# q's weight halves laid 226 columns apart, each with its gate column behind it

## The chip, the cores and the metric

The kernel runs on one core of a Trainium2 chip. The metric is the device time of one execution in microseconds. Three runs of the kernel before gave 392.96, 392.97 and 393.01 us (median 392.97). One more execution, taken with the profiler on, took 392.84 us; its span, from the first to the last recorded instruction, is 391.1 us.

## The reference

Inputs are float32: x of 2048 x 448, the attention's `wqkv` (448 x 1344) and `wo` (448 x 448), the MLP's `w1` (448 x 1792), `b1`, `w2` (1792 x 448) and `b2`, and a gate vector of 448.

```python
g = _sigmoid((x * gate_w).sum(-1, keepdims=True))
a = _A_ref(x, A_wqkv, A_wo)
b = _B_ref(x, B_w1, B_b1, B_w2, B_b2)
return g * a + (1 - g) * b
```

`_A_ref` is attention with 16 heads of 28 numbers: each position looks at itself and at seven earlier positions in steps of two, and the result goes through `wo`. `_B_ref` is `relu(x @ w1 + b1)**2 @ w2 + b2`. What matters here is the first step of `_A_ref`, `qkv = x @ wqkv`, and the gate's dot product of x and `gate_w`. The kernel computes that as one more column of the products with q's weights.

## The kernel before

**Precision and tiles.** Every float32 operand is split into a high part, rounded to the format `fp32r`, and a low part, the rest. A product x·w is the sum of three products on TensorE: high·high, high·low, low·high. The 448 rows of a weight are three blocks of 128 rows (k = 0, 1, 2) and one of 64. For the last block q's weights take partitions 0 to 63 of `w7h` and `w7l`, k's take partitions 64 to 127 of the same columns. The 2048 positions are four chunks of 512, and a chunk is four tiles of 128 positions. x is the stationary operand and the weights are the moving one, so a product's duration goes with the columns of the weights.

**The woven reading.** `woven` (L190) makes the moving operand's access pattern: it takes the columns alternately from two halves (column n of the first half, column n of the second, then n + 1 of both), and `woven_out` (L196) names the output's columns accordingly. For a weight of 448 columns the halves lie 224 columns apart. q's weights have NQ = 450 columns: 448, and twice the gate's column behind them. With halves 224 apart, the gate's column at 448 is reached as number 224 of the second half, and number 224 of the first half is column 224 itself, read a second time. `NH = D // 2 + 2` makes 226 pairs, so that these products have 452 output columns; `qkv_evacuate` takes the gate's value from output column 449 (`pt[:, D + 1:D + 2]`, L369).

**The start.** An order written out by hand stands in L801 to L843. Nineteen products on zeros run first on TensorE. Meanwhile q's weights, `raws[0]`, arrive block by block on SP's queue and x's first chunk in `rx`. For each block k (L830 to L839) ScalarE copies the 450 columns into `wqh` (the high part), VectorE subtracts that from the raw numbers into `wql` (the low part), and both split x in the same way. L840 to L843 do this for the last block. GpSimd has only fills to do at this time (L239, L241, L306).

**The products.** `qkv_first` (L420) runs q's products of chunk 0 in the order in which the blocks come in: for each of the three blocks of 128 rows, over four tiles, high·high, low weights, low x (L429, 36 products on all 128 rows). All later products go through `side_by_side` (L334): each uses 64 rows of the array, and a pair, one in each half of the array, runs at the same time on two different tiles (L341). The last block of q (`last`, L398) runs in pairs with k's. In chunks 1 to 3 `qkv_two` (L447) does two tiles per call in 63 pairs; in such a call the first half has 24 products of q and the second 18, never in the same pair, and the partner is always one of k or v with 448 columns.

**What sets the order behind it.** From L846 on a planner (`Plan`) gives each engine its order at build time from written costs and start times (`START`, `FIRST`, `MM448`). The times are constants in the code, so the planner's order does not depend on how the weights are laid out. `x_load` (L705) brings the next chunks of x into the two buffers of the pool `rawp`; the first of them is the one that held `raws[0]`.

Of the kernel before, what the change touches and what calls it, by code (L numbers as in the profile page):

```python
# [9 lines left out]
AF = mybir.ActivationFunctionType  # L10
# [3 lines left out]
S, D, H, DH, W, F = 2048, 448, 16, 28, 8, 1792  # L14
# [7 lines left out]
NF = F // P  # L22
CH = 512
NQ = D + 2
NH = D // 2 + 2
NP = 512


# [155 lines left out]
def gated_mix_kernel(ctx: ExitStack, tc: tile.TileContext, xT, wqkv, w1, w2, wo, b1, b2, out):  # L184
    nc = tc.nc

    def f32(ap):
        return ap.bitcast(F32)

    def woven(w):  # L190

        if w.shape[1] == NQ:
            return bass.AP(tensor=w.tensor, offset=w.offset, ap=[list(w.ap)[0], [1, NH], [D // 2, 2]])
        return w.rearrange("p (i n) -> p n i", i=2)

    def woven_out(pt, n):  # L196
        return (pt[:, :2 * NH] if n == NQ else pt[:, :n]).rearrange("p (n i) -> p n i", i=2)

# [81 lines left out]
    def x_slot(j, o=16):  # L280
        return x_place[0][:, o + 2 * CH * j:o + 2 * CH * (j + 1)].rearrange("p (i n) -> p i n", i=2)

    def x_tiles(c):
        if c % 2:
            x_place[0] = xpool.tile([P, 8 * CH + 16], F32R, tag="x", name=f"x{c}")
            return [x_slot(j, 0 if c == 1 else 16) for j in range(4)]
        return [xap.tile([P, 2, CH], F32R, tag=f"x{j}", name=f"x{c}_{j}") for j in range(4)]
# [9 lines left out]
    ap = actx.enter_context(tc.tile_pool(name="phase_a", bufs=1, reuse_waits="tile"))  # L297
    xap = actx.enter_context(tc.tile_pool(name="phase_a_x", bufs=1, reuse_waits="tile"))
    wqh = ap.tile([P, 3, NP + 2 * D], F32R, name="wqh")
    wql = ap.tile([P, 3, NP + 2 * D], F32R, name="wql")  # L300
    w7h = ap.tile([P, NP + D], F32R, name="w7h")
    w7l = ap.tile([P, NP + D], F32R, name="w7l")
# [10 lines left out]
    def ncols(b):  # L313
        return NQ if b == 0 else D

    def block(b):
        o = (0, NP, NP + D)[b]
        return slice(o, o + ncols(b))
# [15 lines left out]
    def side_by_side(*todo):  # L334
        assert len(todo[0]) == len(todo[1])
        for pair in zip(*todo):
            need(*(j for e in pair for j in (*e[0].after, *e[3:])))
            for r, (acc, a, w, *_) in enumerate(pair):
                rows = slice(r * 64, r * 64 + 64)
                assert acc.rows in (None, r)  # L340
                nc.tensor.matmul(woven_out(acc.pt, acc.n), a[rows], woven(w[rows]), start=acc.todo == acc.all, stop=acc.todo == 1)  # L341
                acc.todo, acc.rows, acc.after = acc.todo - 1, r, ()
            plan.pe(MM512 if pair[0][0].n == CH else MM448 + (pair[0][0].n - D) * 1.7)
# [41 lines left out]
    def wqj(b, k):  # L385
        return wq_jobs.get((b, k), ())
# [10 lines left out]

    def last(x, acc, tl, b):  # L398
        sl = slice(tl * P, tl * P + P)
        n = block(1) if b == 2 else slice(0, ncols(b))  # L400
        h, l = w7h[:, n], w7l[:, n]
        (wh, wl), (xh, xl) = (wqj(2, 3) if b == 2 else ()) or (None, None), x.parts[3] or (None, None)
        return [(acc, x.x7[:, sl], h, *filter(None, (wh, xh))), (acc, x.x7[:, sl], l, *filter(None, (wl,))),
                (acc, x.x8[:, sl], h, *filter(None, (xl,)))]
# [15 lines left out]
    def qkv_first(x):  # L420
        four = range(4)
        q = accs(0, 0, four, "bbbb")
        for k in range(3):
            todo = [full(x, q[i], i, 0, (k,)) for i in four]
            for some in ((0, 1), (2, 3)) if k == 0 else (four,):
                for j in range(3):
                    for i in some:
                        acc, a, w, *_ = todo[i][j]
                        nc.tensor.matmul(woven_out(acc.pt, NQ), a, woven(w), start=k == j == 0, stop=False)  # L429
            plan.pe(FIRST[k])  # L430
        for acc in q:
            acc.todo = 3
        k = accs(0, 1, four, "mmmm")
        t = [sum((last(x, a[i], i, b) for i in four), []) for b, a in ((0, q), (1, k))]
        f = [full(x, k[i], i, 1) for i in four]
        run(0, [t[0] + f[0] + f[1] + f[2] + f[3], t[1] + f[2] + f[3] + f[0] + f[1]],
            [(3, [(0, 0, q[0])], (k[0], k[0])),
             (12, [(0, i, q[i]) for i in (1, 2, 3)], (k[1], k[1])),
             (24, [], (k[0], k[2])), (33, [], (k[1], k[3])),
             (39, [(1, 0, k[0]), (1, 2, k[2])]), (48, [(1, 1, k[1]), (1, 3, k[3])])])  # L440
        v = accs(0, 2, four, "bbbb")
        f, l = [full(x, v[i], i, 2) for i in four], [last(x, v[i], i, 2) for i in four]
        run(0, [f[0] + l[0] + f[2] + l[2] + f[1] + f[3], f[1] + l[1] + f[3] + l[3] + f[0] + f[2]],
            [(15, [], (v[0], v[1])), (24, [], (v[2], v[3])),
             (33, [(2, 0, v[0]), (2, 1, v[1])]), (42, [(2, 2, v[2]), (2, 3, v[3])])])

    def qkv_two(x, c, t0, beside=()):  # L447
        t1 = t0 + 1
        kinds = ("mm", "bm", "bb") if beside else ("mm", "mb", "bb")
        (q0, q1), (k0, k1), (v0, v1) = (accs(c, b, (t0, t1), tags) for b, tags in enumerate(kinds))  # L450
        run(c, [full(x, q0, t0, 0) + last(x, q0, t0, 0) + full(x, q1, t1, 0) + last(x, q1, t1, 0) + full(x, k0, t0, 1)
                + full(x, k1, t1, 1) + full(x, v0, t0, 2) + last(x, v0, t0, 2) + full(x, v1, t1, 2),
                full(x, k1, t1, 1) + last(x, k1, t1, 1) + full(x, v0, t0, 2) + full(x, v1, t1, 2) + last(x, v1, t1, 2)
                + full(x, q0, t0, 0) + full(x, q1, t1, 0) + full(x, k0, t0, 1) + last(x, k0, t0, 1)],
            [(24, [], (q0, k1)), (33, [], (q1, v0)), (42, [(0, t0, q0), (1, t1, k1)], (k0, v1)),
             (51, [(0, t1, q1)]), (51, [], *beside[:1]), (54, [(2, t0, v0)]), (57, [], *beside[1:]),
             (63, [(1, t0, k0), (2, t1, v1)])])
# [351 lines left out]
    raws = [rawp.tile([P, 4, 512], F32, tag="raw", name="wqraw0")]  # L809
# [12 lines left out]
    for b, tag in ((1, "k"), (2, "v")):  # L822
        raw = attp.tile([P, 3, D], F32, tag=tag, name=f"wqraw{b}")
# [3 lines left out]
    raw7 = attp.tile([P, D], F32, tag="q", name="wqraw7")  # L827
    nc.sync.dma_start(raw7, wqkv[2, :, 3, :D])
    x = X(x_tiles(0))
    for k in range(3):  # L830
        nc.scalar.activation(wqh[:, k, :NQ], raws[0][:, k, :NQ], AF.Copy)
        for n, cols in enumerate(halves if k == 0 else (slice(0, CH),)):
            if k or n:
                nc.scalar.activation(x.h[k][:, cols], rx[:, k, cols], AF.Copy)
            else:
                nc.vector.tensor_copy(x.h[k][:, cols], rx[:, k, cols])
            if not n:
                nc.vector.tensor_sub(wql[:, k, :NQ], raws[0][:, k, :NQ], f32(wqh[:, k, :NQ]))
            nc.vector.tensor_sub(x.l[k][:, cols], rx[:, k, cols], f32(x.h[k][:, cols]))  # L839
    nc.scalar.activation(w7h[:, :NQ], raws[0][:, 3, :NQ], AF.Copy)  # L840
    nc.vector.tensor_sub(w7l[:, :NQ], raws[0][:, 3, :NQ], f32(w7h[:, :NQ]))
    nc.scalar.activation(x.x7, rx[:, 3], AF.Copy)
    nc.vector.tensor_sub(x.x8, rx[:, 3], f32(x.x7))  # L843

# [304 lines left out]
    def wo_end(st):  # L1149
        for r in range(2):  # L1150
            for e in wo_full(st, r, (0, 1, 2)):
                acc, a, w, *js = e
                need(*acc.after, *js)
                nc.tensor.matmul(woven_out(acc.pt, D), a, woven(w), start=False, stop=acc.todo == 1)  # L1154
                acc.todo, acc.after = acc.todo - 1, ()
                plan.pe(MM448)
            fin_add(st.par, st.t + r, acc, gt[:, st.par, st.t + r:st.t + r + 1])
# [93 lines left out]
    for g in range(2, 2 * NF):  # L1251
        i, f = g // (NF // 2), g % (NF // 2) * 2
# [111 lines left out]
```

## Time and profile before

| | |
|---|---|
| median of three runs | 392.97 us |
| profiled execution | 392.84 us, span 391.1 us |
| TensorE busy | 386.5 us (99%) |
| VectorE busy | 260.3 us (67%) |
| GpSimd busy | 260.6 us (67%) |
| ScalarE busy | 205.4 us (53%) |
| DMA, mean over the span | 189 GB/s |

Times in the profile are microseconds from the span's start. PE is TensorE's products, PEld its weight loads (the stationary operand), DVE is VectorE, ACT ScalarE, POOL GpSimd, SP the engine that issues most of the DMAs; a name with a q behind it is an engine's queue. A row of the timeline has start, duration, engine, line, operation, output <- input, shapes and how many instructions are merged in it; in brackets stands the idle time in front of it and what ended that. A row of a group has the busy time and the mean duration in nanoseconds of one instruction. A product's record reaches to its modelled end, so records of neighbouring products overlap; what a product costs in a stream is seen in the distance of their starts and in the difference between forms.

### The profile page before, as it was taken

The page shows a single profiled execution, that of the slowest core. Times are in us where ns is not written, and L with a number is a line of the kernel's source. Part 1 is how long each engine was busy: PE and PEld are TensorE (multiplying, and loading weights), DVE is VectorE, ACT ScalarE, POOL GpSimd, SP SyncE. Part 2 cuts the span into 40 slices and gives each one's busy share as a digit, 9 for nine tenths or more (in the row PEclk, how much of TensorE's full clock was granted, in tenths as well). Part 3 has the DMA queues.
Part 4 walks back from the last instruction along what each step waited for, and adds up shares of the span by engine and source line. Part 5 has one row for each costly group of instructions (what it writes and reads, how often), then busy time and mean ns, then how long its engine had stood idle before and what let it go on. Part 6 is the DMA issues. An engine that isn't in the chain of part 4 may idle for free.

```text
span 391.1 us, 9273 instructions
## 1 busy us (share of the span) xinstructions
PE 386.5 (99%) x3829; PEld 385.3 (99%) x3829; DVE 260.3 (67%) x346; ACT 205.4 (53%) x501; POOL 260.6 (67%) x165
## 2 busy tenths in 40 slices
PE   9999999999999999999999999999999999999996
PEld 8999999999999999999999999999999999999995
DVE  4525523588585778778656989789666686668454
ACT  5857865362566566445555445345716343456740
POOL 0000003979999989959999887999998979661000
PEclk9999999999999999999999999999999999999999
DMA  7999999997174062644203779645635220226835
GB/s 240 399 356 318 373 369 355 377 340 267 49 253 151 1 219 80 220 167 164 90 2 137 244 209 271 218 112 141 217 106 166 84 96 2 88 64 164 141 106 189
DMA packets 64697, 73.75 MB, mean 189 GB/s; under 512 B 32336, under 2 KB 57488, under 8 KB 64272
## 3 DMA queue, kind: packets, MB, share of 16 engines
q1 hardware_dynamic: 64224, 72.79, 56.4%
q8 instruction: 30, 0.49, 0.5%
q10 hardware_dynamic: 432, 0.38, 0.3%
q14 instruction: 11, 0.09, 0.1%
HBM read 45.71 MB, written 28.25 MB: 189 GB/s over the span
## 4 chain that ended last, share of the span: by engine, by line
PE 99%; DVE 0%; DVEq 0%; issue 0%
PE b L341 33%; PE h L341 32%; PE qkv L341 23%; PE a L341 7%; PE qkv L429 2%; PE warm L807 1%; PE a L1154 1%; DVE bt_b L1037 0%; DVEq L1359 0%
## 5 line engine op out<-in xcount | busy, mean ns | idle before, releaser
L539 POOL TENSOR_TENSOR pp<-q,k 128x896 f32<-128x896 f32 x56 | 116.8, 2119 | 75.1 <-DMA k<-k_d 63.5
L341 PE MATMUL h<-x,w1h 64*128 64x512 f32 x672 | 122.0, 376 | 0.0
L551 POOL TENSOR_TENSOR pp<-lg,v 128x896 f32<-128x896 f32 x64 | 113.9, 1868 | 9.4 <-DVE o L561 5.0
L341 PE MATMUL qkv<-wqh,x 64*128 64x448 f32 (+1 forms) x528 | 83.2, 350 | 0.0
L341 PEld LDWEIGHTS h<-x,w1h 64*128 64x128 f32 x672 | 82.8, 186 | 0.0
L341 PE MATMUL h<-x,w1l 64*128 64x512 f32 x336 | 75.9, 376 | 0.0
L793 DVE TENSOR_TENSOR h<-h,h 128x512 fp32r<-128x512 f32 x56 | 38.7, 691 | 55.1 <-ACT h L792 54.9
L543 DVE TENSOR_REDUCE lg<-pp 128x32 f32<-128x896 f32 x64 | 66.9, 1076 | 12.5 <-POOL pp L539 12.5
L341 PE MATMUL b<-w2bh,h 64*128 64x448 f32 x448 | 69.5, 349 | 0.0
L341 PE MATMUL b<-w2ah,h 64*128 64x448 f32 x448 | 69.2, 349 | 0.0
L561 DVE TENSOR_REDUCE o<-pp 128x112 f32<-128x896 f32 x64 | 67.5, 1066 | 0.0
L341 PEld LDWEIGHTS qkv<-wqh,x 64*128 64x128 f32 x528 | 61.0, 186 | 0.0
L341 PE MATMUL qkv<-wql,x 64*128 64x448 f32 (+1 forms) x264 | 56.8, 350 | 0.0
L789 ACT ACTIVATE h<-h,b1z 128x512 f32<-128x512 f32 x56 | 36.7, 655 | 37.1 <-PE h L341 37.1
L341 PEld LDWEIGHTS b<-w2bh,h 64*128 64x128 f32 x448 | 53.2, 193 | 0.0
L341 PEld LDWEIGHTS b<-w2ah,h 64*128 64x128 f32 x448 | 53.1, 193 | 0.0
L341 PE MATMUL b<-w2bl,h 64*128 64x448 f32 x224 | 47.6, 349 | 0.0
L341 PE MATMUL b<-w2al,h 64*128 64x448 f32 x224 | 47.5, 349 | 0.0
L341 PEld LDWEIGHTS h<-x,w1l 64*128 64x128 f32 x336 | 44.0, 186 | 0.0
L791 ACT ACTIVATE h<-h 128x512 fp32r<-128x512 f32 x56 | 33.4, 597 | 1.6
L363 ACT ACTIVATE st<-qkv 128x448 f32<-128x448 f32 x48 | 24.3, 539 | 17.8 <-PE qkv L341 11.5
L341 PEld LDWEIGHTS qkv<-wql,x 64*128 64x128 f32 x264 | 33.2, 186 | 0.0
(108 smaller groups left out, 576.4 us busy)
## 6 DMA issues: line engine op xcount, KB each, us to landing
v<-v_d SPq DMA_DIRECT2D x8, 840.0 KB, 6.8
x_d<-x SPq DMA_DIRECT2D x12, 512.0 KB, 7.3
x<-x_d SPq DMA_DIRECT2D x12, 512.0 KB, 4.1
k<-k_d SPq DMA_DIRECT2D x7, 840.0 KB, 7.4
q_d<-st SPq DMA_DIRECT2D x8, 448.0 KB, 5.8
k_d<-st SPq DMA_DIRECT2D x8, 448.0 KB, 5.7
v_d<-st SPq DMA_DIRECT2D x8, 448.0 KB, 6.4
o_d<-o SPq DMA_DIRECT2D x16, 224.0 KB, 2.1
```

What stands on the lines that cost most here:

```text
L341: nc.tensor.matmul(woven_out(acc.pt, acc.n), a[rows], woven(w[rows]), start=acc.todo == acc.all, stop=acc.todo == 1)
L363: nc.scalar.activation(st[0][:, :, t % 2].rearrange("p (i g) c -> p i g c", i=2), unwoven(pt[:, :D]).rearrange("p i (g c) -> p i g c", c=C ...
L429: nc.tensor.matmul(woven_out(acc.pt, NQ), a, woven(w), start=k == j == 0, stop=False)
L539: nc.gpsimd.tensor_mul(pr.rearrange("p (w c) -> p w c", w=W), q[:, s:s + 1].to_broadcast([P, W, C]), k[:, s:s + W])
L543: nc.vector.tensor_reduce(lgs[i][:, s], pr.rearrange("p (w h d) -> p w h d", w=W, h=HG), axis=AX.X, op=ALU.add)
L551: nc.gpsimd.tensor_mul(pr.rearrange("p (h d w) -> p w h d", h=HG, w=W), lgs[i][:, s][:, :, :, None].to_broadcast([P, W, HG, DH]), vs[i][:, ...
L561: nc.vector.tensor_reduce(o_t[par, s][:, g * C:(g + 1) * C], pr.rearrange("p (c w) -> p c w", w=W), axis=AX.X, op=ALU.add)
L789: a = add(ACT, 656.0, lambda pt=pt, r=r: nc.scalar.activation(pt, pt, AF.Relu, bias=b1t[:, f + r:f + r + 1]), ready, bias_job[0], prio=NEXT)
L791: b = add(ACT, 600.0, lambda pt=pt, hh=hh: nc.scalar.activation(hh, pt, AF.Square), a, prio=NEXT)
L793: low = add(DVE, 690.0, lambda pt=pt, hh=hh, hl=hl: nc.vector.tensor_sub(hl, pt, f32(hh)), a, prio=NEXT)
L807: nc.tensor.matmul(warm[:, :2 * P].rearrange("p (i n) -> p i n", i=2), zero, zeros, start=True, stop=True)
L1154: nc.tensor.matmul(woven_out(acc.pt, D), a, woven(w), start=False, stop=acc.todo == 1)
```

## The change

q's high and low weights get another layout in their tiles: columns 0 to 223 hold the first half, column 224 the gate, columns 226 to 449 the second half and column 450 the gate once more; column 225 is not used. The woven reading of q's weights then has 225 pairs 226 columns apart, 450 output columns. The last block of k, which shares the columns of `w7h` and `w7l` with q's, takes the same layout without the gate; it is passed as a slice of NQ + 1 columns, by which `woven` knows it. The gate's value stays in output column 449. The split of each block is done by two new functions: `wq_high` copies the gate's two columns on GpSimd and the halves on ScalarE, `wq_low` subtracts the gate's two columns on GpSimd and the halves on VectorE. The loads, the tiles' sizes, the planner's costs and all later steps stay.

```diff
-NH = D // 2 + 2
+NH = D // 2 + 1
+NG = NH + 1
...
     def woven(w):
 
-        if w.shape[1] == NQ:
-            return bass.AP(tensor=w.tensor, offset=w.offset, ap=[list(w.ap)[0], [1, NH], [D // 2, 2]])
+        if w.shape[1] in (NQ, NQ + 1):
+            n = NH if w.shape[1] == NQ else D // 2
+            return bass.AP(tensor=w.tensor, offset=w.offset, ap=[list(w.ap)[0], [1, n], [NG, 2]])
         return w.rearrange("p (i n) -> p n i", i=2)
...
     def last(x, acc, tl, b):
         sl = slice(tl * P, tl * P + P)
-        n = block(1) if b == 2 else slice(0, ncols(b))
+        n = block(1) if b == 2 else slice(0, NQ + b)
...
     x = X(x_tiles(0))
+
+    def apart(t):
+
+        t = t[:, :2 * NG].rearrange("p (i n) -> p i n", i=2)
+        return t[:, :, :D // 2], t[:, :, D // 2]
+
+    def wq_high(hi, raw):
+        (q, g), r = apart(hi), raw[:, :D].rearrange("p (i n) -> p i n", i=2)
+        nc.gpsimd.tensor_copy(g, raw[:, D:NQ])
+        nc.scalar.activation(q, r, AF.Copy)
+
+    def wq_low(lo, raw, hi):
+        (q, g), (qh, gh), r = apart(lo), apart(f32(hi)), raw[:, :D].rearrange("p (i n) -> p i n", i=2)
+        nc.gpsimd.tensor_sub(g, raw[:, D:NQ], gh)
+        nc.vector.tensor_sub(q, r, qh)
+
     for k in range(3):
-        nc.scalar.activation(wqh[:, k, :NQ], raws[0][:, k, :NQ], AF.Copy)
+        wq_high(wqh[:, k], raws[0][:, k])
         for n, cols in enumerate(halves if k == 0 else (slice(0, CH),)):
             if k or n:
                 nc.scalar.activation(x.h[k][:, cols], rx[:, k, cols], AF.Copy)
             else:
                 nc.vector.tensor_copy(x.h[k][:, cols], rx[:, k, cols])
             if not n:
-                nc.vector.tensor_sub(wql[:, k, :NQ], raws[0][:, k, :NQ], f32(wqh[:, k, :NQ]))
+                wq_low(wql[:, k], raws[0][:, k], wqh[:, k])
             nc.vector.tensor_sub(x.l[k][:, cols], rx[:, k, cols], f32(x.h[k][:, cols]))
-    nc.scalar.activation(w7h[:, :NQ], raws[0][:, 3, :NQ], AF.Copy)
-    nc.vector.tensor_sub(w7l[:, :NQ], raws[0][:, 3, :NQ], f32(w7h[:, :NQ]))
+    wq_high(w7h, raws[0][:, 3])
+    wq_low(w7l, raws[0][:, 3], w7h)
```

## The prediction

> **What bounds the kernel now.** I read the page's first part and its chain of waits, to see which engine sets the end.
>
> ```profile
> span 391.1 us, 9273 instructions
> PE 386.5 (99%) x3829; PEld 385.3 (99%) x3829; DVE 260.3 (67%) x346; ACT 205.4 (53%) x501; POOL 260.6 (67%) x165
> PE 99%; DVE 0%; DVEq 0%; issue 0%
> ```
>
> The chain that ended last is TensorE (PE) almost alone, so time is won or lost only where PE's stream gets shorter or waits. The chain in order of time tells how early that begins:
>
> ```profile
> 5.18 7.10 PE qkv L429 x36
> 12.28 86.71 PE qkv L341 x911
> ```
>
> From 5.18 on these are products of q, k and v, and nothing else stands between them. The view of waits for the first 13 us has two entries for PE's weight loads in this stretch (columns: waiter, what it waited for, us in total, times, longest):
>
> ```profile
> PEld qkv L341 <- ACT wqh L256: 0.3, 1, 0.3
> PEld qkv L429 <- DVE wql L838: 0.2, 1, 0.2
> ```
>
> For the rest of the span the same view of PE is empty, and the one of its weight loads has a single entry of 0.3 us in the last stage. So a product that gets cheaper early in the kernel moves everything behind it forward, and a wait put into PE's first microseconds moves everything back by the same amount. Both parts of this change lie there: q's products, and the splitting of q's weights that feeds the first of them.
>
> **Part 1: two columns less in each of q's products.** Groups of PE's instructions by shape (the last figure of a row but one is the mean ns of one instruction, its pipeline's tail included):
>
> ```profile
> L341 PE MATMUL h<-x,w1h 64*128 64x512 f32 x672 | 122.0, 376 | 0.0
> L341 PE MATMUL qkv<-wqh,x 64*128 64x448 f32 x384 | 80.8, 349 | 0.0
> L341 PE MATMUL qkv<-wqh,x 64*128 64x452 f32 x144 | 41.9, 351 | 0.0
> L341 PE MATMUL qkv<-wql,x 64*128 64x452 f32 x72 | 25.3, 351 | 0.0
> L341 PE MATMUL qkv<-w7h,x 64*128 64x452 f32 x32 | 10.9, 354 | 0.0
> L341 PE MATMUL qkv<-w7l,x 64*128 64x452 f32 x16 | 5.6, 351 | 0.0
> L429 PE MATMUL qkv<-wqh,x 128*128 128x452 f32 x24 | 5.5, 360 | 0.0
> L429 PE MATMUL qkv<-wql,x 128*128 128x452 f32 x12 | 3.0, 363 | 0.0
> ```
>
> A column costs (376 - 349) / (512 - 448) = 0.42 ns, and 452 columns stand where this slope puts them (349 + 4 x 0.42 = 351). Two columns are 0.84 ns. The products with 452 columns are 36 over all 128 rows, one after another, and 144 + 72 + 32 + 16 = 264 over 64 rows, each beside a product of 448 columns in the other half of the array. The 36 save 36 x 0.84 = 0.03 us. What the 264 save depends on how tightly the halves are tied. By the code, 12 + 6 x 24 = 156 of them run in the first half and 6 x 18 = 108 in the second, never two at once. If every pair waits for its slower member, all 264 count: 0.22 us. If the halves run free and the one with more of them ends last, 156 count: 0.13 us; if the other one does, 108: 0.09 us. I take 0.13, the middle one, because 448 columns beside 452 have kept their 349 ns. Part 1 then gives -0.16 us, between -0.12 and -0.25.
>
> The read pattern itself changes too: a product takes its columns alternately from two places, and these lie 226 columns apart instead of 224. The rows above have two distances, 256 columns (512-column form) and 224, both at the same slope; no row has one that isn't a multiple of 32. I take no cost, as 224 and 256 agree, and keep the case as a rival.
>
> **Part 2: the split of the weights.** Here stand VectorE's and ScalarE's first instructions (start, duration, engine and line):
>
> ```profile
> 4.40 0.29 DVE L836 CAST x<-xraw 128x256 fp32r<-128x256 f32 x1 [3.54 <-DMA xraw<-xT]
> 4.84 0.63 DVE L838 TENSOR_TENSOR wql<-wqraw,wqh 128x450 fp32r<-128x450 f32 x1
> 5.38 0.42 DVE L839 TENSOR_TENSOR x<-xraw,x 128x256 fp32r<-128x256 f32 x1
> 6.00 0.42 DVE L839 TENSOR_TENSOR x<-xraw,x 128x256 fp32r<-128x256 f32 x1 [0.20 <-ACT x L834]
> 6.47 0.63 DVE L838 TENSOR_TENSOR wql<-wqraw,wqh 128x450 fp32r<-128x450 f32 x1
> ...
> 7.62 0.62 DVE L838 TENSOR_TENSOR wql<-wqraw,wqh 128x450 fp32r<-128x450 f32 x1
> 8.74 0.69 DVE L839 TENSOR_TENSOR x<-xraw,x 128x512 fp32r<-128x512 f32 x1 [0.50 <-ACT x L834]
> 9.45 0.63 DVE L841 TENSOR_TENSOR w7l<-wqraw,w7h 128x450 fp32r<-128x450 f32 x1
> ```
> ```profile
> 4.22 0.58 ACT L831 ACTIVATE wqh<-wqraw 128x450 fp32r<-128x450 f32 x1 [1.27 <-DMA wqraw<-wqkv]
> ...
> 5.88 0.56 ACT L831 ACTIVATE wqh<-wqraw 128x450 fp32r<-128x450 f32 x1
> ...
> 8.83 0.58 ACT L840 ACTIVATE w7h<-wqraw 128x450 fp32r<-128x450 f32 x1
> ```
>
> The four copies and the four subtractions keep their engines and lose 2 of 450 columns: about 2 ns each, nothing. New are eight GpSimd instructions on 128x2 numbers, a copy and a subtraction for each block of weights. The rows nearest in size and kind:
>
> ```profile
> 1.21 0.18 POOL L306 MEMSET halo<- 56x112 f32 x1
> L594 POOL TENSOR_TENSOR lg<-lg,mx 128x256 f32<-128x256 f32 x8 | 5.2, 645 | 0.8 <-DVE mx L590 0.8
> L1356 POOL MEMSET const-float32-1.0<- 128x1 f32 x1 | 0.1, 108 | 0.0
> ```
>
> One costs at least the 0.11 us of the smallest fill and at most the 0.65 us of 256 columns; two columns are nearest to the former, so I take 0.15 us. GpSimd has been idle since 1.21 + 0.18 = 1.39 us and gets nothing else before its attention work, so the price counts only where PE, VectorE or SP waits for it.
>
> PE's stream and what it needs:
>
> ```profile
> 5.52 0.65 PE L429 MATMUL qkv<-wql,x 128*128 128x452 f32 x2
> 6.01 0.93 PE L429 MATMUL qkv<-wqh,x 128*128 128x452 f32 x4
> ...
> 7.15 1.31 PE L429 MATMUL qkv<-wqh,x 128*128 128x452 f32 x6
> 8.30 0.93 PE L429 MATMUL qkv<-wql,x 128*128 128x452 f32 x4
> 9.06 1.69 PE L429 MATMUL qkv<-wqh,x 128*128 128x452 f32 x8
> ```
>
> - First block, high part. GpSimd's copy can start with ScalarE's at 4.22, as both wait for one load, and ends near 4.4; ScalarE ends at 4.80. Hidden by 0.4 us.
> - First block, low part. GpSimd's subtraction follows its own copy, some 4.45 to 4.6, but VectorE's cast runs from 4.40 to 4.69 and its subtraction from 4.84 to 5.47. If the two engines exclude each other, GpSimd goes in the gap, 4.70 to 4.85, and VectorE starts up to 0.05 us late. PE waits for this subtraction (5.47 to 5.52), and behind it PE runs without a gap, so a delay here goes straight to the end. Bounds: 0, and 0.25 us if GpSimd comes only behind the subtraction (5.47 + 0.15, plus some 0.1 for the hand-overs). I take +0.04.
> - Second block. Its load is there by 5.88 at the latest; the first four products with it start behind the second and third products of the 7.15 row, near 7.53, and those with its low part at 8.30. ScalarE ends at 6.44, VectorE at 7.10: over a microsecond is spare, which covers GpSimd's 0.15 twice and a delay of VectorE as well. Without that cover it would be rival A.
> - Third and fourth block: products near 9.8 and 10.6, and behind 12.2. VectorE rests from 8.24 to 8.74; nothing.
> - The second x chunk's load goes into the buffer that holds q's raw weights, so SP now waits for GpSimd's last subtraction too:
>
> ```profile
> 10.11 1.40 SPq L653 DMA_DIRECT2D xraw<-xT  x2
> L715 ACT ACTIVATE x<-xraw x4: 612/612/612, 18.5 to 20.0; 128x512 fp32r<-128x512 f32 x4
> ```
>
> If GpSimd finds no room between 8.74 and 10.08, its last two run to about 10.4 and the load goes out 0.3 us late. Queued behind it on SP is only the other chunk's load, which already left a microsecond later (two in 1.40 us). The chunk is converted at 18.5 and multiplied behind chunk 0's 48 + 42 pairs, at about 12.2 + 90 x 0.19 = 29 us. Hidden.
>
> PE also waits for one more engine at each block; such a wait is in no view here. The first load of weights started 0.06 us behind ScalarE's end (4.80 to 4.86); I bound it by 0 and 0.06 and count it within the 0.04.
>
> The lock has a row of its own:
>
> ```profile
> 88.36 1.54 DVE L698 TENSOR_TENSOR w2al<-w2raw,w2ah 128x1344 fp32r<-128x1344 f32 x1
> 88.52 3.35 POOL L539 TENSOR_TENSOR pp<-qk 128x896 f32<-128x896 f32 x1 [2.96 <-DVE lg L543]
> L539 POOL TENSOR_TENSOR pp<-q,k 128x896 f32<-128x896 f32 x56 | 116.8, 2119 | 75.1 <-DMA k<-k_d 63.5 <-DVE lg L543 7.6 <-DVE o L561 3.9
> ```
>
> A GpSimd product of 2.12 us took 3.35 when it met a VectorE subtraction, 1.23 us more, about what was left of that (88.36 + 1.54 - 88.52 = 1.38): GpSimd stood still until VectorE was through. [...]
>
> **The sum** is made against the profiled execution, 392.84 us (391.1 us of span and 1.7 around it): 392.84 - 0.16 + 0.04 = 392.72. The runs' median, 392.97, is 0.13 above it, so the forecast is 392.85 us, 0.03% below before. A measurement of this kernel tells 0.2%, 0.79 us, from no change; this is within.
>
> **Rivals.**
> A. VectorE starves GpSimd. The first subtraction on GpSimd waits out 4.84 to 5.80 and runs in the next gap until 5.95, so PE resumes near 6.0 instead of 5.52 (+0.5). The second block's copy then misses the gap before 6.00; from there to 8.24 VectorE has none over 0.05 us, the copy ends near 8.4, and PE, due at 7.53, is 0.9 us late altogether: 392.97 + 0.9 - 0.16 = 393.7. For it: the lock row. Against it: GpSimd asks before VectorE at 4.4 and has 4.69 to 4.84 free.
> B. The writes are put in one order: ScalarE's copy and VectorE's subtraction write around the gate's column, and if the overlap is judged by whole stretches each waits for GpSimd's instruction in front, 0.2 us (0.15 and a hand-over) each in the first block: 393.2. Against it: no byte is shared.
> C. The odd distance slows q's reads, and the kernel with it. At worst the second half goes at half speed, 225 x 0.42 = 95 ns a product; with one column time lost in four, 24 ns, and 36 + 156 products in the half that counts: 192 x 24 ns = 4.6 us, 397.4 us in all. It decides from 0.95 us / 192 = 5 ns a product (to eat part 1 and pass 0.2%). For it: nothing in the trace has read at such a distance. Against it: the slope is one for both distances that are there.
> [...]
> D. The columns bring nothing, as the 448-column neighbour sets each pair's pace: 392.97 + 0.04 - 0.03 = 392.98.
>
> **Chances.** Forecast 0.72 (its own range 392.7 to 393.0), D 0.08, A 0.07, B 0.05, C 0.08. Forecast, D and B are within 0.2%; A ends at 393.7, beside the bound of 393.76, and I give a third of it to slower; C is slower. That makes slower 0.10, same 0.88, and 0.02 is left for faster, for which I see no mechanism. The range, 392.6 to 393.4, takes in the ends of both parts (-0.25, and +0.25 with -0.12) and B; A and C stay out.
>
> **What would show it.** Right: the 450-column rows at about 350 ns, 36 and 264 of them; GpSimd's eight rows near 0.15 us from 4.2 us on; PE's row of 5.52 within 0.05 us; no new wait of PE. The chain of products from 12.28 on starts at the same time and ends 0.1 to 0.2 us sooner. Wrong: PE's weight load waiting for POOL (A or B: the rows at 5.52 and 7.53 tell which), or a 450-column row above 352 ns (C).

## The result, and the profile after

| | before | after |
|---|---|---|
| median | 392.99 us (392.96 to 393.51, 6 runs) | 395.69 us (394.14 to 397.11, 6 runs) |
| profiled execution | 392.84 us, span 391.1 us | 395.44 us, span 393.7 us |
| ratio after / before | | 1.0063, 95% interval 1.0048 to 1.0078 |

The changed kernel is slower: by the ratio 0.63%, and the two medians lie 2.7 us apart. The forecast was 392.85 us with a range up to 393.4. From the page of the profile after, the engines' busy time and the chain of waits by engine:

```profile
PE 388.1 (99%) x3829; PEld 386.2 (98%) x3829; DVE 262.4 (67%) x346; ACT 205.6 (52%) x501; POOL 262.5 (67%) x173
PE 97%; DMA 1%; ACT 0%; DVE 0%; DVEq 0%; issue 0%; ACTq 0%
```

Before, TensorE had 99% of this chain, and only its own products on zeros stood in front of q's. Now a load has 1% and ScalarE appears. The chain in order of time shows them (start, duration, what):

```profile
0.75 3.71 DMA wqraw<-wqkv
...
4.48 0.02 ACTq L841
...
4.53 1.19 ACT L841
...
5.82 0.59 ACT wqh L841
...
6.45 8.86 PE qkv L431 x36
15.31 86.58 PE qkv L343 x911
...
386.57 3.62 PE a L1172 x18
...
390.21 0.45 DVE bt_b L1055
```

And the same view of before, its last products:

```profile
383.67 3.62 PE a L1154 x18
...
387.31 0.45 DVE bt_b L1037
```

The last products start 386.57 - 383.67 = 2.90 us later. (The span grew by 2.6 only: behind VectorE's last piece it goes on for 393.7 - 390.21 = 3.5 us after and 391.1 - 387.31 = 3.8 before.) The rows split the 2.90:

- The 36 products of chunk 0 start at 6.45 in this chain instead of 5.18: +1.27.
- They take 8.86 us instead of 7.10: +1.76. (By the timeline the first of them started at 4.97 before, while the last product on zeros was still on record. Counted from there the start is 1.48 later and the stretch 1.55 longer, 8.86 instead of 12.28 - 4.97 = 7.31.)
- From the first 64-row pair to the last 18 products it is 386.57 - 15.31 = 371.26 us instead of 383.67 - 12.28 = 371.39: -0.13. That is all the change gains, and it is there.

So 3.03 us are lost before 15.31. The timeline of that stretch, after:

```profile
4.51 0.19 POOL L840 CAST wqh<-wqraw 128x2 fp32r<-128x2 f32 x1 [3.12 <-DMA wqraw<-wqkv]
4.53 1.28 ACT L841 ACT_TABLE_LOAD   x1 [4.53 <-DMA wqraw<-wqkv]
...
5.82 0.58 ACT L841 ACTIVATE wqh<-wqraw 128x448 fp32r<-128x448 f32 x1
...
6.45 1.12 PE L431 MATMUL qkv<-wqh,x 128*128 128x450 f32 x2 [1.28 <-ACT wqh L841]
6.48 0.20 POOL L845 TENSOR_TENSOR wql<-wqraw,wqh 128x2 fp32r<-128x2 f32 x1 [1.78 <-ACT wqh L841]
...
6.71 0.63 DVE L846 TENSOR_TENSOR wql<-wqraw,wqh 128x448 fp32r<-128x448 f32 x1 [1.75 <-POOL wql L845]
...
7.39 1.12 PE L431 MATMUL qkv<-wql,x 128*128 128x450 f32 x2
...
8.30 1.69 PE L431 MATMUL qkv<-wqh,x 128*128 128x450 f32 x4
...
8.74 0.46 POOL L845 TENSOR_TENSOR wql<-wqraw,wqh 128x2 fp32r<-128x2 f32 x1 [0.69 <-ACT wqh L841]
...
9.80 0.57 PE L431 MATMUL qkv<-wql,x 128*128 128x450 f32 x2
```

The same view of before has these two rows; the prediction did not read the first:

```profile
1.67 1.28 ACT L831 ACT_TABLE_LOAD   x1 [1.67 <-PEq L1356]
...
4.97 0.69 PE L429 MATMUL qkv<-wqh,x 128*128 128x452 f32 x2
```

Three things are to be seen.

**ScalarE's table load.** It takes 1.28 us in both kernels. Before, it ran at 1.67, while the weights were still on their way. After, it runs at 4.53, released by the weights' load, and the first copy and the first product stand behind it. What has come in between is the queue's entry at 4.48: ScalarE's first copy now depends on two things, the load and GpSimd's copy. In the trace this entry is a wait for the load's semaphore by itself, and the copy at 5.82 carries the wait for GpSimd's; before, the copy at 4.22 carries the wait for the load, and no such entry stands in front of the table load. (The load itself landed later in this execution, 4.48 instead of 4.22 at ScalarE; that is 0.26 of the 1.48 us.)

**A chain of engines.** GpSimd's subtraction (6.48) was released by ScalarE's copy and VectorE's (6.71) by GpSimd's, though each writes columns that the other doesn't touch. VectorE's subtraction starts 0.31 us behind the end of ScalarE's copy (5.82 + 0.58 = 6.40 to 6.71); before it was 0.04 (4.80 to 4.84). First product to first low-part product is 7.39 - 6.45 = 0.94 us instead of 0.55 (4.97 to 5.52), but these products also ran at the slow pace that comes next.

**Slow products.** The four products from 8.30 to 9.80 start 0.375 us apart. The six that stood at 7.15 to 8.30 in the kernel before started 0.19 us apart. The view by stretches (stretch, its length, busy time and number of instructions of PE, PEld, DVE, ACT and POOL, then the granted TensorE clock, the DMA share and GB/s) has 6 products in 1.70 us, where before has 11 (its row stands with the second experiment), and yet a clock of 1.00:

```profile
7.50:9.20 1.70, 1.70 (x6) 1.55 (x6) 1.64 (x4) 1.53 (x3) 1.01 (x4) 1.00 0.90 236
```

The clock's own entries in the trace say why. The first one, full clock, begins at 9.853 us in this execution and at 5.210 in that of before, and the column reads 1.00 ahead of it as well. The products on zeros (256 columns each) show the pace there: they start 0.213 us apart ahead of the first entry and 0.112 behind it (in the repeated execution below, where it comes at 3.792). So in this execution TensorE didn't lose its full clock by resting; it got it 4.6 us later. The groups of products by shape say the same (the last figure but one is the mean ns of one):

```profile
L431 PE MATMUL qkv<-wqh,x 128*128 128x450 f32 x24 | 6.7, 416 | 1.3 <-ACT wqh L841 1.3
L431 PE MATMUL qkv<-wql,x 128*128 128x450 f32 x12 | 3.5, 407 | 0.0
L343 PE MATMUL qkv<-wqh,x 64*128 64x450 f32 x144 | 41.8, 350 | 0.0
```

The early 36 went from 360 and 363 ns to 416 and 407; the later ones, at 350, are where the prediction put them. The waits of TensorE in the first 14 us name the releasers:

```profile
PE qkv L431 <- ACT wqh L841: 1.3, 1, 1.3
PEld qkv L431 <- DVE wql L846: 0.4, 1, 0.4
```

From 14 us on the view has no wait of TensorE's products and two entries of 0.3 us of its weight loads; all of the loss is in front.

### The profile page after: what moved, and what is told of

Same layout as the page of the kernel before. It is cut to its first block, busy times and chain, and to the rows that moved or that the text cites. A ratio compares the mean times of both kernels' runs of the same rounds, so it can differ in the third digit from the quotient of the medians.

```text
span 393.7 us, 9287 instructions
## 1 busy us (share of the span) xinstructions
PE 388.1 (99%) x3829; PEld 386.2 (98%) x3829; DVE 262.4 (67%) x346; ACT 205.6 (52%) x501; POOL 262.5 (67%) x173
## 4 chain that ended last, share of the span: by engine, by line
PE 97%; DMA 1%; ACT 0%; DVE 0%; DVEq 0%; issue 0%; ACTq 0%
PE b L343 32%; PE h L343 32%; PE qkv L343 23%; PE a L343 7%; PE qkv L431 2%; DMA wqraw<-wqkv 1%; PE a L1172 1%; ACT L841 0%; ACT wqh L841 0%; DVE bt_b L1055 0%; DVEq L1377 0%; ACTq L841 0%
## 5 line engine op out<-in xcount | busy, mean ns | idle before, releaser
L343 PE MATMUL h<-x,w1h 64*128 64x512 f32 x672 | 116.6, 376 | 0.0
L343 PEld LDWEIGHTS h<-x,w1h 64*128 64x128 f32 x672 | 74.1, 186 | 0.0
L343 PE MATMUL h<-x,w1l 64*128 64x512 f32 x336 | 69.3, 376 | 0.0
L343 PEld LDWEIGHTS qkv<-wqh,x 64*128 64x128 f32 x528 | 57.3, 186 | 0.0
L343 PEld LDWEIGHTS b<-w2bh,h 64*128 64x128 f32 x448 | 48.0, 193 | 0.0
L343 PEld LDWEIGHTS b<-w2ah,h 64*128 64x128 f32 x448 | 47.9, 192 | 0.0
L343 PE MATMUL b<-w2al,h 64*128 64x448 f32 x224 | 43.2, 349 | 0.0
L343 PE MATMUL b<-w2bl,h 64*128 64x448 f32 x224 | 43.2, 349 | 0.0
L343 PEld LDWEIGHTS h<-x,w1l 64*128 64x128 f32 x336 | 37.4, 186 | 0.0
L794 ACT ACTIVATE h<-h 128x512 f32<-128x512 f32 x56 | 33.1, 591 | 0.0
```

The lines of the kernel that those rows point to most:

```text
L794: a = add(ACT, 600.0, lambda pt=pt: nc.scalar.activation(pt, pt, AF.Square), b, prio=NEXT)
```

## The experiments

The theory, T, as it stood before the experiments: the shared stretch of columns makes an order ScalarE, GpSimd, VectorE; ScalarE's first copy thereby gets a second wait, the table load falls behind the weights' load, and TensorE, idle for more than a microsecond, loses its full clock. Its rivals stand in the expectations.

### The table load brought forward

On the kernel after. ScalarE gets a small activation on one unused number at the start; the table load then stands in front of that and not behind the wait. The order of the engines stays.

```diff
         nc.scalar.dma_start(rx[:, 0, cols], xT[0, :, 0, cols])
+    nc.scalar.activation(b1z[0:1, 14:15], none, AF.Copy)
```

> The changed kernel with one ScalarE copy of a single number put in front, which waits for no load, so that ScalarE's table load (1.28 us) can run before the weights arrive. Theory (T): the loss of 2.7 us has three links. First, ScalarE's first copy has two things to wait for, the load and GpSimd's copy of the gate, and its table load now stands behind the first of these waits, at 4.53 instead of 1.67 us. Second, ScalarE, GpSimd and VectorE run one after another in each block, 0.2 us each hand-over. Third, TensorE's idle time of 1.3 us lets its clock fall to half for some us. T expects the table load near 1.7 us, the first product near 5.2, the first product with the low part 0.8 behind it, the idle time mostly gone and the clock kept: 393.1 to 393.6 us. If the order of the three engines alone is the cause (R1, the prediction's rival B), nothing of it changes: 395 to 396 us. If it is the odd distance of the halves (R2, rival C), 395.7 us too.

Measured: 393.07 us (392.99 to 394.46, 12 runs), ratio 0.9997, interval 0.9988 to 1.0005 (the kernel before 393.23 beside it, 25 runs). Its timeline:

```profile
1.67 1.28 ACT L816 ACT_TABLE_LOAD   x1 [1.67 <-PEq L1375]
...
4.59 0.58 ACT L842 ACTIVATE wqh<-wqraw 128x448 fp32r<-128x448 f32 x1 [1.43 <-POOL wqh L841]
...
5.22 1.12 PE L431 MATMUL qkv<-wqh,x 128*128 128x450 f32 x2
5.25 0.20 POOL L846 TENSOR_TENSOR wql<-wqraw,wqh 128x2 fp32r<-128x2 f32 x1 [0.69 <-ACT wqh L842]
...
5.47 0.63 DVE L847 TENSOR_TENSOR wql<-wqraw,wqh 128x448 fp32r<-128x448 f32 x1 [0.66 <-POOL wql L846]
...
6.16 0.91 PE L431 MATMUL qkv<-wql,x 128*128 128x450 f32 x2
```

The table load is back at 1.67, the first product at 5.22, and the 2.7 us are gone; R1 and R2, which expected 395 us and more, fall. The chain of engines is still there: ScalarE waits for GpSimd, GpSimd for ScalarE, VectorE for GpSimd, and VectorE's subtraction starts 0.30 us behind the copy's end (4.59 + 0.58 = 5.17 to 5.47). The low part comes 0.94 us behind the first product (0.8 was expected); the clock's first entry is at 6.713 in this execution, so the products between ran at the slow pace, and these 0.94 us are not the chain's price. In the median that price can't be told from nothing. (The profiled execution is the 394.46 of the 12; its first 64-row pair starts at 13.14 in the chain instead of 12.28, and TensorE's products wait 0.9 us for ScalarE at 60 us, their weight load 1.3. The others end at 393.34 or below.)

### Two waits without the new layout

On the kernel before. GpSimd fills one column of the first block's high weights (which ScalarE's copy then overwrites), so that this copy waits for GpSimd as well. Nothing else changes.

```diff
     x = X(x_tiles(0))
+    nc.gpsimd.memset(f32(wqh[:, 0, NQ - 1:NQ]), 0.0)
     for k in range(3):
         nc.scalar.activation(wqh[:, k, :NQ], raws[0][:, k, :NQ], AF.Copy)
```

> The kernel before, with one thing added: GpSimd fills one number of the first block's high part before ScalarE's copy overwrites it. The fill is done by 1.5 us and nobody is held up by it, but ScalarE's first copy now has two engines to wait for. T: the table load moves behind the load's landing, to about 4.3 us; the first product comes 1.3 to 1.5 us later, near 6.3; the clock is lost for a part of the first products; the low part follows the first product by the 0.55 us of before at full clock. 394.3 to 396.0 us, and runs that differ by more than 1 us. R1 and R2: 393.0 us, as there is neither a new order nor a new layout.

Measured: 395.30 us (394.44 to 396.13, 4 runs), ratio 1.0050, interval 1.0032 to 1.0069. Its timeline:

```profile
4.38 1.28 ACT L832 ACT_TABLE_LOAD   x1 [4.38 <-DMA wqraw<-wqkv]
...
6.31 0.65 PE L429 MATMUL qkv<-wqh,x 128*128 128x452 f32 x2 [1.61 <-ACT wqh L832]
6.97 0.69 PE L429 MATMUL qkv<-wql,x 128*128 128x452 f32 x2
```

GpSimd's fill was over long before; the mere presence of a second wait moved the table load from 1.67 to 4.38. With old columns, no chain (first product to low part 0.66 us) and eight GpSimd instructions fewer, most of the loss is there, where R1 and R2 expected 393.0. The view by stretches of this kernel:

```profile
7.50:9.20 1.70, 1.70 (x6) 1.54 (x5) 1.70 (x5) 1.27 (x4) 0.00 (x0) 0.50 0.90 256
```

The same stretch of the kernel before:

```profile
7.50:9.20 1.70, 1.70 (x11) 1.68 (x10) 1.20 (x3) 1.00 (x2) 0.00 (x0) 1.00 1.01 271
```

The clock is 0.50, and TensorE gets 6 products through where it got 11. Here the full clock had been granted (its first entry is at 4.037) and was taken back at 7.450. The four runs lie at 394.44, 394.48, 396.11 and 396.13, with mean granted clocks of 1.0, 0.999, 0.994 and 0.994: the two longer ones have that stretch of half clock.

### The same waits with TensorE kept busy

On the kernel after. Only the number of products on zeros in front changes, so that TensorE doesn't rest while ScalarE loads its table.

```diff
-WARM = 19
+WARM = 31
```

> The changed kernel with 31 warm-up products instead of 19, so that TensorE works until its first operands are there. T: the waits stay (first product near 6.5 us, low part 0.7 to 0.9 later), but the products that follow run at 0.19 us each instead of 0.37: about 1.2 us less than 395.7, 394.2 to 394.8 us, and the runs agree within 0.5 us instead of 3. If the clock is not part of it (R3), 395.7 us and the same spread.

Measured: 394.22 us (394.16 to 394.85, 6 runs), ratio 1.0027, interval 1.0016 to 1.0038. Its timeline:

```profile
4.34 1.28 ACT L841 ACT_TABLE_LOAD   x1 [4.34 <-DMA wqraw<-wqkv]
...
7.27 0.54 PE L431 MATMUL qkv<-wqh,x 128*128 128x450 f32 x2
...
```

And its chain of waits:

```profile
7.43 6.84 PE qkv L431 x36
```

The products on zeros lasted longer than meant, as they run at the slow pace themselves (the first entry of the clock is at 6.965), so that the first real one came at 7.27 and not near 6.5. From there the 36 products take 6.84 us, 0.19 each, where after needs 8.86: the slow pace is worth 2.0 us against the full one, and 1.55 of after's loss, as before also starts slowly. By the medians the kernel is 395.69 - 394.22 = 1.47 us faster than after (1.4 by the two ratios) although its first product is 0.8 us later; R3 falls. What is left over the kernel before is the late start: the first 64-row pair comes at 7.43 + 6.84 = 14.27 in this chain instead of 12.28. The spread of the six runs went from 3.0 us to 0.7 (0.5 was expected).

### No shared stretch

On the kernel after. Each of the four instructions of a block is cut in two, so that every one writes adjoining columns and no engine's stretch contains another's. Twice as many instructions, the same bytes.

```diff
-        nc.gpsimd.tensor_copy(g, raw[:, D:NQ])
-        nc.scalar.activation(q, r, AF.Copy)
+        for i in range(2):
+            nc.gpsimd.tensor_copy(g[:, i:i + 1], raw[:, D + i:D + i + 1])
+            nc.scalar.activation(q[:, i], r[:, i], AF.Copy)
...
-        nc.gpsimd.tensor_sub(g, raw[:, D:NQ], gh)
-        nc.vector.tensor_sub(q, r, qh)
+        for i in range(2):
+            nc.gpsimd.tensor_sub(g[:, i:i + 1], raw[:, D + i:D + i + 1], gh[:, i:i + 1])
+            nc.vector.tensor_sub(q[:, i], r[:, i], qh[:, i])
```

> The changed kernel with the same engines for the same columns, but each of the four instructions of a block cut in two at the gate's columns: halves of 224 columns and single gate columns, so that no operand's stretch from first to last column holds another engine's column. T, carried one step back: ScalarE's second wait comes from judging overlap by whole stretches; without it the first copy waits for the load alone, so the table load is back near 1.67 us with no help, GpSimd no longer waits for ScalarE, nor VectorE for GpSimd. First product near 5.1 (two copies of 224 columns take some 0.1 us more than one of 448), low part 0.6 to 0.8 behind it, 392.8 to 393.4 us. If GpSimd's part itself is what costs (the lock of the prediction's rival A, now with twice as many GpSimd instructions), above 394.5 us.

Measured: 393.19 us (392.76 to 393.56, 11 runs), ratio 0.9998, interval 0.9990 to 1.0007. Its timeline:

```profile
1.67 1.28 ACT L842 ACT_TABLE_LOAD   x1 [1.67 <-PEq L1376]
...
4.48 0.67 ACT L842 ACTIVATE wqh<-wqraw 128x224 fp32r<-128x224 f32 x2 [1.53 <-DMA wqraw<-wqkv]
4.51 0.30 POOL L841 CAST wqh<-wqraw 128x1 fp32r<-128x1 f32 x2 [3.12 <-DMA wqraw<-wqkv]
...
4.90 0.69 DVE L848 TENSOR_TENSOR wql<-wqraw,wqh 128x224 fp32r<-128x224 f32 x2
...
5.25 0.62 PE L431 MATMUL qkv<-wqh,x 128*128 128x450 f32 x2 [0.43 <-ACT wqh L842]
...
5.74 0.62 PE L431 MATMUL qkv<-wql,x 128*128 128x450 f32 x2
...
7.31 0.97 POOL L847 TENSOR_TENSOR wql<-wqraw,wqh 128x1 fp32r<-128x1 f32 x2
```

ScalarE's copy (4.48) and GpSimd's (4.51) now start together, both released by the load alone, and the table load is back at 1.67 with nobody having asked for it. That the order came from the stretches, not from the bytes, is thereby shown: the bytes are the same. The first product comes at 5.25 (near 5.1 was expected), the low part 0.49 us behind it (0.6 to 0.8). GpSimd does sixteen instructions here, some of them held up (0.97 us for two), and no cost of it shows in the time; GpSimd's own time and the lock are out as causes of the loss. (The view of waits puts 0.6 us of the first weight load, ending at 5.22, down to GpSimd's subtraction; the product behind it doesn't read that, and its own wait, 0.43 us, is for ScalarE.)

### The kernel after once more, beside it

> The changed kernel once more, on the chip of the run above and against the same runs of before. T: 1.004 to 1.008 of before, runs that differ by over 1 us; its profile has the table load behind the first weights' landing.

Measured on the same chip as the last one: 395.55 us (394.17 to 395.81, 6 runs), ratio 1.0047, interval 1.0033 to 1.0062. The timeline has its first product at 6.40, behind 1.83 us of rest:

```profile
6.40 0.65 PE L431 MATMUL qkv<-wqh,x 128*128 128x450 f32 x2 [1.83 <-ACT wqh L841]
...
7.34 1.12 PE L431 MATMUL qkv<-wql,x 128*128 128x450 f32 x2 [0.29 <-DVE wql L846]
```

The first two products ran at full clock here, and TensorE then waited 0.29 us for VectorE: the chain of engines, seen by itself.

The clock's own entries in the trace, in us, for this run and for the one with two waits:

```
after, repeated     half clock  7.205 to 10.618, full from 3.792 to 7.205 and again from 10.618
before, two waits   half clock  7.450 to 10.863
```

The half clock lasts 3.413 us in both. At 0.375 us a product instead of 0.19 that is 3.413 / 0.375 = 9.1 products, each 0.185 us late, 1.7 us in all: the distance between the two groups of runs of the kernel with two waits (396.12 - 394.46 = 1.66).

The half pace thus comes in two forms, and the kernel after has both. Of its six runs only the one of 395.75 us has a mean granted clock of 0.994. The others have 0.998 to 1.0, also those of 395.44, 395.63, 395.79 and 397.11 us. The profiled one, 395.44, had its early products at half pace because the full clock came only at 9.853; the other three have no trace.

### The layout without the split by engines

On the kernel after. The host lays out q's weights (and the last block of k's) with the gate's column behind each half and a column of zeros between; a block is one ScalarE copy and one VectorE subtraction of 451 columns, and GpSimd has no part in it.

```diff
+NL = 2 * NG - 1
...
-                nc.sync.dma_start(raws[0][rows, k, :NQ], wqkv[b, rows, k])
+                nc.sync.dma_start(raws[0][rows, k, :NL], wqkv[b, rows, k])
...
-        wq_high(wqh[:, k], raws[0][:, k])
+        nc.scalar.activation(wqh[:, k, :NL], raws[0][:, k, :NL], AF.Copy)
...
-                wq_low(wql[:, k], raws[0][:, k], wqh[:, k])
+                nc.vector.tensor_sub(wql[:, k, :NL], raws[0][:, k, :NL], f32(wqh[:, k, :NL]))
...
+    def apart(w):
+        return _np.concatenate([w[:, :D // 2], gw, gap, w[:, D // 2:], gw], 1)
```

> The new layout without the new instructions: the host stacks q's weights (and the last rows of k's) with the gate's column behind each half and a column of zeros between, rows of 451 numbers; one ScalarE copy and one VectorE subtraction of 451 columns for each block, nothing on GpSimd. T: table load at 1.67 us, first product near 5.0, 450 columns in q's products: the kernel before less part 1 of the prediction, 392.8 to 392.9 us. R2 (the odd distance costs): above 393.0 us, by as much as the distance costs.

Measured: 393.08 us (392.81 to 393.29, 11 runs), ratio 0.9995, interval 0.9986 to 1.0004. Its chain of waits:

```profile
5.18 7.19 PE qkv L432 x36
12.36 7.76 PE qkv L344 x76
...
383.62 3.62 PE a L1157 x18
```

From the first pair to the last 18 products it is 383.62 - 12.36 = 371.26 us, to the hundredth what it is after, and 0.13 less than before. The chains of the run without a shared stretch (383.70 - 12.44) and of the one with TensorE kept busy (385.53 - 14.27) have the same 371.26, and the one with two waits and the old columns (386.80 - 15.41) the 371.39 of before. The profiled execution took 392.81 us; the median, expected at 392.8 to 392.9, came 0.2 higher, on a chip where the kernel before scattered from 392.93 to 394.13 around 393.23. That is above the 393.0 which the expectation set for R2, but not above the kernel before beside it, and the stretch of 371.26 leaves no room for a cost of the distance. So no cost of the layout itself is to be seen: 450 columns at a distance of 226 gain their 0.13 us in the chain. The time can't tell that: no version was measurably faster than before.

## Why the prediction was wrong, step by step

- **What bounds the kernel: right.** A wait in TensorE's first microseconds goes to the end: 3.03 us were lost before 15.31, and 2.90 arrive.
- **Part 1, the columns: right.** 371.39 to 371.26 us over the 264 paired products is the -0.13 that was taken (156 products of 0.84 ns), and it came out alike in the four profiles with 450 columns given above. The 36 early products were to give 0.03 more. The rows agree: before starts 28 of them from 6.01 to 11.35, 190.7 ns each, and the run with TensorE kept busy takes 6.84 us for 36, 190.0 ns each.
- **The odd distance (rival C): no cost.** 450 columns at distance 226 take 350 ns, where 448 take 349. The 24 ns a product behind C's 397.4 us were the author's estimate; no run shows them: these rows are 1 ns apart.
- **Part 2, the step that failed: "The four copies and the four subtractions keep their engines and lose 2 of 450 columns: about 2 ns each, nothing."** Their durations did stay (0.58 and 0.63 us). Their waits didn't. The prediction had GpSimd's copy and ScalarE's start together, "as both wait for one load"; but ScalarE's copy got a second wait, for GpSimd's, and the table load, which had been hidden under the weights' transfer, came out from under it: 1.28 us. The copy starts 0.01 us behind the load (4.53 + 1.28 = 5.81, 5.82). The prediction listed what each instruction costs and on whom TensorE waits, but not what the first instruction on ScalarE pulls along in front of it; the row at 1.67 was in the same view of ScalarE that was quoted from 4.22 on.
- **"such a wait is in no view here ... I bound it by 0 and 0.06": wrong bound.** TensorE waited 1.3 us for ScalarE, and its weight load 0.4 us for VectorE (0.2 before).
- **GpSimd's instructions: mis-sized by little.** 0.15 us was taken, 0.19 (copy) and 0.20 (subtraction) were measured in the first block. Where one met a VectorE subtraction it took 0.46 (the row at 8.74; VectorE's subtraction of x ran from 8.46 to 9.14): the lock is real, and the slack behind the first block covers it, as the prediction said. Rival A falls: no wait of TensorE from the second block on, neither in after nor in the run without a shared stretch, whose products come at the full pace from 6.20 us on.
- **Rival B named the cause and missed its price.** The writes are put in one order by whole stretches; "no byte is shared" was no argument against it, as the run without a shared stretch shows (ScalarE's copy at 4.48 and GpSimd's at 4.51, both released by the load alone). It was given 0.2 us per hand-over, 0.4 in all and 5%. The way over GpSimd is of that size (VectorE's subtraction 0.31 instead of 0.04 us behind ScalarE's copy; 0.29 us of TensorE's waiting in the repeated execution), and in the run with the early table it can't be told from nothing in the time. What B lacked was the table load (1.28 us) and the slow pace (1.55 us more for the 36 products).
- **The clock was no term at all.** The prediction put a stall of TensorE at its own length. Here an idle time of 1.3 to 1.8 us went with 3.4 us of products at half pace, and that cost about as much again (1.55 to 1.7 us): in the profiled execution of after because the full clock came only at 9.853 us instead of 5.210, in the two executions with 1.6 and 1.8 us because it had come and was taken back for 3.413 us.
- **Range and chances.** Of the rivals only C, at its worst, reached past 395.7, by a mechanism that the runs don't show; A stood at 393.7 and B at 393.2. B with the table load alone would have been 393.2 + 1.3 = 394.5, near the fastest runs of after and of the kernel with two waits (394.14 to 394.48).

What stays open: what the chain of engines costs by itself (between nothing and the 0.29 us of the repeated execution), what decides when the full clock comes, and why one run of after took 397.11 us. A full clock that came some 3.4 us later still than in the profiled execution would make up its 1.67 us more (9 products of 0.185 us); that run has no trace, so this is not shown.

## What to carry to other kernels

When an instruction moves to another engine, write down the waits of everything that writes near it, judged from first to last column, and look at the first instruction of each engine: what stands in front of it and has so far been hidden (here a table load) may fall behind a new wait. If two engines must write into one tile, give them adjoining stretches, or start the table load with an instruction that waits for nothing; either brought the kernel back to the time before (ratios 0.9997 and 0.9998). A stall of TensorE so near the start is to be priced with the slow clock that went with it here (1.3 us of idle time, and 1.55 us more for the 36 products), not by its own length.

## What the runs showed of the hardware

- All eight profiled executions begin at the slow pace (products on zeros 0.213 us apart); the full clock comes between 3.792 and 9.853 us, and ahead of that the profile's clock column reads 1.00 all the same.
- TensorE went to half clock after resting 1.8 of the 3.4 us before (the row of the repeated kernel after: full from 3.792 to 7.205, first product at 6.40 after 1.83 us of rest), and stayed there 3.413 us, though its products came without a rest from 7.34 on. The run with two waits has the same 3.413 us, from 7.450 to 10.863, behind 1.61 us of rest up to 6.31. A rest of 0.43 us behind the first entry at 4.299 (the run without a shared stretch) brought no half clock.
- When the stretch of half clock begins depends on the run: at 7.450 us in the profiled run with two waits and 7.205 in the repeated one. The runs of the three kernels with the late table load and 19 products on zeros spread by 1.6 to 3.0 us, the six with TensorE kept busy by 0.7 us, the kernel before on the same chip by 1.2 us over 25 runs.
